# One attention chain across the token groups, with values and scores taking turns on TensorE

## The chip, the cores and the metric

The kernel runs on one core of one Trainium2 chip. The metric is the device time of one execution in microseconds (us); what is compared is the median over several executions.

## What is computed

Three layers follow one another, all in float32. The attention is cut into chunks of 64 tokens, so each chunk of each head sees only itself; its output feeds a dense mixture of 4 experts, and that feeds a mixture of 8 experts in which each token takes one expert.

```python
# q, k, v: (4, 8, 576, 64), cut along the sequence into chunks of 64
scores = scale * np.matmul(q_c, k_c.transpose(0, 1, 2, 4, 3))
scores = scores - np.max(scores, axis=-1, keepdims=True)
attn = np.exp(scores)
attn = attn / (np.sum(attn, axis=-1, keepdims=True) + 1e-09)
out = np.matmul(attn, v_c)
...
x = attn_out.transpose(0, 2, 1, 3).reshape(B * S, H * D)      # 2304 tokens x 512
x = _moe_ref(x=x, **moe_kwargs)        # 4 experts, all tokens through each, weighted
return _moe2_ref(x=x, **moe2_kwargs)   # 8 experts, each token through the one it scores highest
```

## The kernel before

The 2304 tokens are 18 tiles of 128 tokens, and a tile holds two chunks of 64. The tiles form seven groups of 2, 3, 3, 3, 3, 2 and 2 (`GROUPS`). The first mixture works group by group: for each expert it takes eight steps (`chunk`), each of which multiplies the group's tokens with one 128-wide slice of the hidden layer (`ffn1`, L358 to L360) and then, for the step before, with the second weight matrix (`ffn2`, L418). Every float32 operand there is split into a high and a low part, which is why each product appears three times. Two groups share one pass over the weights (`SUPER`), so the steps run in the order group 0, then 1 and 2, then 3, then 4 and 5, then 6.

The attention of a group is done in pieces that are put between these steps. For one tile the pieces are:

- scores (`att_scores`, L186): 8 heads times 2 chunks, 16 matmuls of 64x64x64. The two chunks lie on the two halves of the partitions, so their operands and results use either partitions 0 to 63 or 64 to 127. All results go to one PSUM bank. VectorE then takes the maximum (L192) and subtracts it (L193), and ScalarE exponentiates (L197).
- normalisation (`att_norm`, L202 to L206): VectorE alone.
- transposes (`att_transpose`, L214): four 128x128 transposes into one PSUM bank, copied out by ScalarE (L216, `aT`).
- values (`att_values`, L237): again 16 matmuls of 64x64x64 into one PSUM bank; ScalarE copies the result out as `xh` (L244), VectorE makes the rest `xl` (L245). When a tile's values are done its input buffer is free, and the load of the tile four further on is queued for two steps later.

Scores, transposes and values all take their bank from one ring of two PSUM banks (`ps("m")`), in the order of the program. `att_pieces(g)` lists the pieces of group g. For all groups but the first, a piece can hold the values of tile i-2 (all 16 matmuls) followed by the scores of tile i (all 16), then come the transposes of tile i-1, then the normalisation of tile i. At the start of a group there are no values to go with the scores of its first two tiles, and at its end no scores to go with the values of its last two: a group of n tiles has n+2 such pieces. `plan` spreads the pieces of a group evenly over at most 24 steps that end just before the group is first needed. Group 0 has a list of its own, done before the first step. A piece that is the first of its step stands on TensorE between that step's `ffn1` and the `ffn2` of the step before; a further piece of the same step comes after that `ffn2`.

Of the kernel before, what the change touches and what calls it, by code (L numbers as in the profile page):

```python
# [1 line left out]

# [15 lines left out]
P = 128  # L18
NT = 2304
NTILE = NT // P  # L20
# [7 lines left out]
CH = 64  # L28
# [28 lines left out]
def attn_moe_moe2(ctx, tc, att, probs, wg, wgt, w12, m2w, out):  # L57
# [17 lines left out]
    def ps(tag):  # L75
        return ring(psum, "ps_" + tag, {"h": 2, "o": 4, "m": 2}[tag], [P, 512], F32)
# [89 lines left out]
    def heads(t, half):  # L166

        if t < GROUPS[0]:
            return slice(4 * half, 4 * half + 4), 4
        return (slice(0, H), H) if half else None  # L170

    def att_scores(t, half):

        a = atin[t]
        if half == 0:
            live[t] = [
                sds[t % 2],
                apool.tile([P, 2, H], F32, tag="mx", name=f"mx{t}"),
                None,
            ]  # L180
        if half == 0 or t < GROUPS[0]:
            live[t][2] = ps("m").rearrange("p (h x) -> p h x", x=CH)
        sd, mx, sc = live[t]
        for g in range(4 * half, 4 * half + 4):
            for c in (slice(0, CH), slice(CH, P)):
                nc.tensor.matmul(  # L186
                    sc[c, g, :], lhsT=a[c, 512 + g * CH:512 + (g + 1) * CH], rhs=a[c, g * CH:(g + 1) * CH],
                    start=True, stop=True,
                )
        if heads(t, half):  # L190
            hs, n = heads(t, half)
            nc.vector.tensor_reduce(out=mx[:, 0, hs].unsqueeze(2), in_=sc[:, hs, :], axis=AX.X, op=ALU.max)  # L192
            nc.vector.tensor_tensor(  # L193
                out=sd[:, hs, 0:CH], in0=sc[:, hs, :], in1=mx[:, 0, hs].unsqueeze(2).to_broadcast([P, n, CH]),
                op=ALU.subtract,
            )
            nc.scalar.activation(sd[:, hs, 0:CH], sd[:, hs, 0:CH], AF.Exp, scale=0.125)  # L197

    def att_norm(t, half):
        sd, mx, _ = live[t]  # L200
        hs, n = heads(t, half)
        nc.vector.tensor_reduce(out=mx[:, 1, hs].unsqueeze(2), in_=sd[:, hs, :], axis=AX.X, op=ALU.add)  # L202
        nc.vector.reciprocal(mx[:, 1, hs], mx[:, 1, hs])
        if hs.start == 0:
            live[t][2] = apool.tile([P, H, CH], F32, tag="pn", name=f"pn{t}")
        nc.vector.tensor_tensor(  # L206
            out=live[t][2][:, hs, :], in0=sd[:, hs, 0:CH], in1=mx[:, 1, hs].unsqueeze(2).to_broadcast([P, n, CH]), op=ALU.mult
        )

    def att_transpose(t):  # L210
        sdf = live[t][2].rearrange("p h k -> p (h k)")
        pt = ps("o" if t < GROUPS[0] else "m")
        for i in range(4):
            nc.tensor.transpose(pt[:, i * P:(i + 1) * P], sdf[:, i * P:(i + 1) * P], ident)  # L214
        aT = apool.tile([P, 512], F32, tag="aT", name=f"aT{t}")
        nc.scalar.copy(aT, pt)  # L216
        live[t] = aT

    def att_values(t, half, g):
        a = atin[t]  # L220
        if g not in xs:
            n = GROUPS[g] * P
            xs[g] = (
                xpool.tile([P, KD, n], F32R, tag="xh", name=f"xh{g}"),
                xpool.tile([P, KD, n], F32R, tag="xl", name=f"xl{g}"),
            )
        xh, xl = xs[g]
        off = (t - starts[g]) * P
        if half == 0:
            live[t] = [live[t], None]  # L230
        if half == 0 or t < GROUPS[0]:
            live[t][1] = ps("o" if t < GROUPS[0] else "m")
        aT, pv = live[t]
        for q in range(4 * half, 4 * half + 4):
            w = slice(q * CH, (q + 1) * CH)
            for c in (slice(0, CH), slice(CH, P)):
                nc.tensor.matmul(  # L237
                    pv[c, w], lhsT=a[c, 1024 + q * CH:1024 + (q + 1) * CH], rhs=aT[c, w], start=True, stop=True,
                )
        if heads(t, half):  # L240
            hs, n = heads(t, half)
            ks = slice(hs.start // 2, hs.stop // 2)
            pvv = pv.rearrange("p (k x) -> p k x", x=P)[:, ks, :]
            nc.scalar.copy(xh[:, ks, off:off + P], pvv)  # L244
            nc.vector.tensor_tensor(out=xl[:, ks, off:off + P], in0=pvv, in1=xh[:, ks, off:off + P].bitcast(F32),  # L245
                                    op=ALU.subtract)
        if half == 1:
            live.pop(t)
            atin.pop(t)
            if t + NATT < NTILE:  # L250
                attq.append((t + NATT, stream["call"] + 2 if stream["call"] else 0))

    def att_pieces(g):

        a = starts[g]
        n = GROUPS[g]
        S = lambda i, h: (lambda: att_scores(a + i, h))
        N = lambda i, h: (lambda: att_norm(a + i, h))
        T = lambda i: (lambda: att_transpose(a + i))
        V = lambda i, h: (lambda: att_values(a + i, h, g))  # L260
        if g == 0:
            return [S(0, 0), S(0, 1), N(0, 0), S(1, 0), N(0, 1), S(1, 1), T(0), N(1, 0), N(1, 1), V(0, 0), V(0, 1),
                    T(1), V(1, 0), V(1, 1)]


        pcs = []
        for i in range(n + 2):
            both = []
            if i >= 2:
                both += [V(i - 2, 0), V(i - 2, 1)]  # L270
            if i < n:
                both += [S(i, 0), S(i, 1)]
            pcs.append(lambda both=both: [p() for p in both])
            if 1 <= i <= n:
                pcs.append(T(i - 1))
            if i < n:
                pcs.append(N(i, 1))
        return pcs


# [592 lines left out]
    for g in range(1, len(GROUPS)):  # L873
        free = lastuse[g - NX] + 2 if g >= NX else 0
        end = first[g] - (1 if g < len(GROUPS) - 1 else KF + 1)
        begin = max(at, free, end - 24)
        pcs = att_pieces(g)
        for i, p in enumerate(pcs):
            plan.setdefault(begin + i * (end - begin) // len(pcs), []).append(p)
        at = end  # L880
# [40 lines left out]
    for t in range(3, NATT):  # L921
        att_load(t)
    pieces = att_pieces(0)

    warm = zero.bitcast(BF16)[:, 0:512]
# [117 lines left out]
def _layouts(q, k, v, moe_domain_probs, moe_w1, moe_w2, moe2_w_gate, moe2_w1, moe2_w2):  # L1043
# [16 lines left out]
    def chunks(w1, w2):  # L1060
        n = w1.shape[0]
        a = w1.reshape(n, KD, P, KF, P).transpose(0, 3, 2, 1, 4).reshape(n, KF, P, KD * P)
        return np.concatenate([a, w2.reshape(n, KF, P, D)], axis=-1)

    return [att, probs, wg, moe2_w_gate.T, chunks(moe_w1, moe_w2), chunks(moe2_w1, moe2_w2)]

# [17 lines left out]
```

## Time and profile before

| | |
|---|---|
| median of 3 executions | 1174.14 us (1174.12 to 1174.23) |
| the profiled execution, its own time | 1172.4 us |
| its span, first to last instruction | 1170.3 us |
| mean granted TensorE clock | 0.998 |
| TensorE (PE) busy | 1146.9 us, 98% of the span |
| VectorE (DVE) busy | 694.1 us, 59% |
| ScalarE (ACT) busy | 480.6 us, 41% |

The profile is one execution, seen by the hardware profiler. PE is TensorE's matmul row and PEld its weight loads, which run beside matmuls. An instruction is named by its line in the kernel, its engine, its operation and `out<-in`; `64*64 64x64` for a matmul means 64 rows and 64 columns of the array in use and 64 columns streamed. A float32 matmul shows as two records, each a weight load and a matmul, so the 16 matmuls of one tile's scores are 32 records. Matmul records overlap, since their ends are modelled; the distance from one start to the next is what TensorE takes for one.

### The profile page before, as it was taken

To read this page: it belongs to the slowest core of one execution; us is meant where nothing else is said; L and a number is where in the kernel's file an instruction comes from. 1 tells how busy PE (TensorE), PEld (TensorE's weight loads), DVE (VectorE), ACT (ScalarE), POOL (GpSimd) and SP (SyncE) were. 2 spreads that over 40 slices of the span, in tenths; PEclk is the share of its full clock that TensorE was granted. 3 is DMA by queue.
4 is the path that set the end of the run, shared out by engine and by line. 5 is a ranking of instruction groups with operands and counts; after the bars stand their busy time and mean duration, and the time that the engine had idled before them with its cause. 6 is when DMAs were issued, how large, how long until landed. Compare 5 with 4: busy or idle time off the path is not lost. (4 is left out here: it accounts for less than half of the span.)

```text
span 1170.3 us, 19108 instructions
## 1 busy us (share of the span) xinstructions
PE 1146.9 (98%) x7447; PEld 1027.7 (88%) x7447; DVE 694.1 (59%) x1370; ACT 480.6 (41%) x801; POOL 97.6 (8%) x125
## 2 busy tenths in 40 slices
PE   6999999999999999999999999999999999999996
PEld 5998899999999999988899999988898899888885
DVE  6766735233443666667363746266866765788872
ACT  5544323131221334333141414145445555677771
POOL 0000000000000000100010001001102211222220
PEclk9999999999999999999999999999999999999999
DMA  8657513031131443444031304046763586686850
GB/s 321 202 204 289 190 44 127 2 108 37 54 117 55 156 139 120 137 152 159 22 110 36 126 19 127 21 159 178 200 245 126 202 319 214 203 279 241 288 205 18
DMA packets 52293, 174.14 MB, mean 149 GB/s; under 512 B 10718, under 2 KB 11358, under 8 KB 52064
## 3 DMA queue, kind: packets, MB, share of 16 engines
q1 hardware_dynamic: 46240, 156.54, 39.8%
q0 software_dynamic: 5952, 16.28, 4.1%
q8 instruction: 61, 1.00, 0.4%
q14 instruction: 40, 0.33, 0.1%
HBM read 162.61 MB, written 11.36 MB: 149 GB/s over the span
## 5 line engine op out<-in xcount | busy, mean ns | idle before, releaser
L364 DVE SCALAR_TENSOR_TENSOR hl<-ps_h,hh 128x256 fp32r<-128x256 f32 (+1 forms) x272 | 132.3, 486 | 360.4 <-ACT hh L363 355.6
L363 ACT ACTIVATE hh<-ps_h 128x256 fp32r<-128x256 f32 (+1 forms) x272 | 118.2, 434 | 544.7 <-PE ps_h L360 537.2
L418 PE MATMUL ps_o<-wh,hh 128*128 128x512 f32 x840 | 325.5, 398 | 0.0
L418 PE MATMUL ps_o<-wl,hh 128*128 128x512 f32 (+1 forms) x784 | 305.8, 391 | 0.0
L317 DVE TENSOR_TENSOR wl<-raw,wh 128x1024 fp32r<-128x1024 f32 x212 | 259.3, 1223 | 57.8 <-ACT wh L316 56.8
L358 PE MATMUL ps_h<-xh,wh 128*128 128x384 f32 (+1 forms) x896 | 282.8, 316 | 0.0
L360 PE MATMUL ps_h<-xh,wl 128*128 128x384 f32 (+1 forms) x896 | 280.7, 313 | 0.8 <-DVE wl L317 0.8
L359 PE MATMUL ps_h<-xl,wh 128*128 128x384 f32 (+1 forms) x896 | 280.7, 313 | 0.6 <-DVE xl L245 0.5
L418 PE MATMUL ps_o<-wh,hl 128*128 128x512 f32 x672 | 262.2, 390 | 0.0
L316 ACT CAST wh<-raw 128x1024 fp32r<-128x1024 f32 x212 | 220.7, 1042 | 4.0 <-DMA raw<-in_w 4.0
L418 PEld LDWEIGHTS ps_o<-wh,hh 128*128 128x128 f32 x840 | 157.7, 188 | 25.9 <-ACT x L783 0.5
L358 PEld LDWEIGHTS ps_h<-xh,wh 128*128 128x128 f32 x896 | 168.3, 188 | 9.7 <-DVE wl L317 0.4
L359 PEld LDWEIGHTS ps_h<-xl,wh 128*128 128x128 f32 x896 | 168.3, 188 | 9.0 <-DVE xl L245 1.0
L360 PEld LDWEIGHTS ps_h<-xh,wl 128*128 128x128 f32 x896 | 168.3, 188 | 1.0 <-DVE wl L317 1.0
L418 PEld LDWEIGHTS ps_o<-wl,hh 128*128 128x128 f32 (+1 forms) x784 | 144.5, 184 | 20.1
L418 PEld LDWEIGHTS ps_o<-wh,hl 128*128 128x128 f32 x672 | 126.1, 188 | 27.5
L375 PE MATMUL ps_h<-x,wh 128*128 128x384 f32 x224 | 66.6, 357 | 0.8 <-ACTq L1031 0.8
L471 DVE CUSTOM_DVE_ANT_0 junk<-y,wgb 128x512 bf16<-128x512 f32 x96 | 65.7, 684 | 0.1
L358 PE MATMUL ps_h<-x,wh 128*128 128x256 f32 x192 | 54.6, 284 | 1.8 <-DVEq L1031 1.6
L376 PE MATMUL ps_h<-x,wl 128*128 128x192 f32 x224 | 56.1, 250 | 0.0
L360 PE MATMUL ps_h<-x,wl 128*128 128x256 f32 x192 | 53.9, 281 | 0.0
L359 PE MATMUL ps_h<-x,wh 128*128 128x256 f32 x192 | 53.9, 281 | 0.0
(187 smaller groups left out, 916.2 us busy)
## 6 DMA issues: line engine op xcount, KB each, us to landing
raw<-in_w SPq DMA_DIRECT2D x160, 512.0 KB
raw<-in_m2w SPq DMA_DIRECT2D x52, 512.0 KB
raw_xh<-in_m2w SPq DMA_DIRECT2D x27, 512.0 KB
raw_xl<-in_m2w SPq DMA_DIRECT2D x27, 512.0 KB
atin<-in_att SPq DMA_DIRECT2D x16, 768.0 KB
ytok<-y POOLq DMA_DIRECT2D x18, 256.0 KB, 3.4
wgb<-in_wgt SPq DMA_DIRECT2D x1, 2048.0 KB
atin<-in_att SPq DMA_DIRECT2D x4, 256.0 KB
```

The source lines that it names most:

```text
L316: nc.scalar.copy(wh, raw)
L317: lows.append(lambda: nc.vector.tensor_tensor(out=wl, in0=raw, in1=wh.bitcast(F32), op=ALU.subtract))
L358: nc.tensor.matmul(hp[:, :n], lhsT=w_h, rhs=xh(k), start=(k == 0), stop=False)
L359: nc.tensor.matmul(hp[:, :n], lhsT=w_h, rhs=xl(k), start=False, stop=False)
L360: nc.tensor.matmul(hp[:, :n], lhsT=w_l, rhs=xh(k), start=False, stop=(k == KD - 1))
L363: nc.scalar.activation(hh, hp[:, :n], AF.Relu)
L364: nc.vector.scalar_tensor_tensor(out=hl, in0=hp[:, :n], scalar=0.0, in1=hh.bitcast(F32), op0=ALU.max, op1=ALU.subtract)
L375: nc.tensor.matmul(hp[:, :2 * n], lhsT=wh[:, c], rhs=x[:, k, :, :n], start=(k == 0), stop=False)
L376: nc.tensor.matmul(hp[:, :n], lhsT=wl[:, c], rhs=x[:, k, 0, :n], start=False, stop=(k == KD - 1))
L418: nc.tensor.matmul(y, lhsT=l, rhs=r, start=(fc == 0 and q == 0), stop=(fc == KF - 1 and q == len(parts) - 1))
L471: nc.vector.tensor_tensor_reduce(out=junk, in0=tiles[i], in1=wgb[:, e, :], scale=1.0, scalar=0.0, op0=ALU.mult, op1=ALU.add, accum_out=lg[ ...
```

## The change

Three things change. The group boundary goes: `att_pieces` now lists, for tile i of a group, its transposes, the normalisation of tile i+1, and one piece with the values of tile i and the scores of tile i+2, whether or not tile i+2 belongs to the next group. Group 1 starts the chain with the scores of its first two tiles alone; the last two tiles of all have values alone. Inside such a piece, values and scores are generators that take turns: two matmuls of values (one on each half of the partitions), then two of scores, eight times, and only then the instructions on the other engines, those of the values first. And the scores of a chunk that sits on partitions 0 to 63 are written to partitions 64 to 127 of their bank, and the other way round; the values undo this by reading the other one of each pair of 64-wide columns of `aT` (`q ^ 1`).

```diff
+    def other(c):
+        return slice(P - c.stop, P - c.start)
+
+    def run(*parts):
+        parts = list(parts)
+        while parts:
+            for p in list(parts):
+                try:
+                    next(p)
+                except StopIteration:
+                    parts.remove(p)
...
                 nc.tensor.matmul(
-                    sc[c, g, :], lhsT=a[c, 512 + g * CH:512 + (g + 1) * CH], rhs=a[c, g * CH:(g + 1) * CH],
+                    sc[other(c), g, :], lhsT=a[c, 512 + g * CH:512 + (g + 1) * CH], rhs=a[c, g * CH:(g + 1) * CH],
                     start=True, stop=True,
                 )
+            yield
...
         for q in range(4 * half, 4 * half + 4):
-            w = slice(q * CH, (q + 1) * CH)
+            w, r = [slice(i * CH, (i + 1) * CH) for i in (q, q ^ 1)]
             for c in (slice(0, CH), slice(CH, P)):
                 nc.tensor.matmul(
-                    pv[c, w], lhsT=a[c, 1024 + q * CH:1024 + (q + 1) * CH], rhs=aT[c, w], start=True, stop=True,
+                    pv[c, w], lhsT=a[c, 1024 + q * CH:1024 + (q + 1) * CH], rhs=aT[c, r], start=True, stop=True,
                 )
+            yield
...
-        S = lambda i, h: (lambda: att_scores(a + i, h))
+        S = lambda i, h: (lambda: run(att_scores(a + i, h)))
+        S8 = lambda i: joined(att_scores(a + i, 0), att_scores(a + i, 1))
+        V8 = lambda i: joined(att_values(a + i, 0, g), att_values(a + i, 1, g))
-        V = lambda i, h: (lambda: att_values(a + i, h, g))
+        V = lambda i, h: (lambda: run(att_values(a + i, h, g)))
...
-        pcs = []
-        for i in range(n + 2):
-            both = []
-            if i >= 2:
-                both += [V(i - 2, 0), V(i - 2, 1)]
-            if i < n:
-                both += [S(i, 0), S(i, 1)]
-            pcs.append(lambda both=both: [p() for p in both])
-            if 1 <= i <= n:
-                pcs.append(T(i - 1))
-            if i < n:
-                pcs.append(N(i, 1))
+        pcs = [lambda: run(S8(0)), N(0, 1), lambda: run(S8(1))] if g == 1 else []
+        for i in range(n):
+            pcs.append(T(i))
+            if a + i + 1 < NTILE:
+                pcs.append(N(i + 1, 1))
+            pcs.append(lambda i=i: run(V8(i), *([S8(i + 2)] if a + i + 2 < NTILE else [])))
         return pcs
```

(`joined` is `itertools.chain`.)

## Rows read from the trace of the kernel before

**Rows 1.** The page, busy time by engine: us, share of the span, instructions.
```profile
PE 1146.9 (98%) x7447; PEld 1027.7 (88%) x7447; DVE 694.1 (59%) x1370; ACT 480.6 (41%) x801; POOL 97.6 (8%) x125
```
**Rows 2.** Waits of TensorE from 20 to 760 us: total, times, longest.
```profile
PE ps_h L360 <- DVE wl L317: 0.8, 1, 0.8
```
**Rows 3.** The ps_m tile's instructions, 20 to 760 us: scores and values.
```profile
L186 PE MATMUL ps_m<-atin x512: 218/218/267, 38.0 to 682.6; 64*64 64x64 f32 x171
L237 PE MATMUL ps_m<-aT,atin x512: 218/218/267, 68.9 to 737.7; 64*64 64x64 f32 x171
```
**Rows 4.** Timeline of TensorE around scores alone: start us, us, instruction.
```profile
37.34 0.28 PE L359 MATMUL ps_h<-xl,wh 128*128 128x256 f32 x1
...
37.80 0.28 PE L360 MATMUL ps_h<-xh,wl 128*128 128x256 f32 x1
38.01 1.15 PE L186 MATMUL ps_m<-atin 64*64 64x64 f32 x32
...
39.42 0.40 PE L418 MATMUL ps_o<-wl,hh 128*128 128x512 f32 x1
```
**Rows 5.** Timeline of TensorE around values alone.
```profile
90.87 0.28 PE L360 MATMUL ps_h<-xh,wl 128*128 128x256 f32 x1
91.08 1.15 PE L237 MATMUL ps_m<-aT,atin 64*64 64x64 f32 x32
...
92.49 0.40 PE L418 MATMUL ps_o<-wl,hh 128*128 128x512 f32 x1
```
**Rows 6.** Timeline of TensorE around values followed by scores.
```profile
68.69 0.28 PE L360 MATMUL ps_h<-xh,wl 128*128 128x256 f32 x1
68.90 1.15 PE L237 MATMUL ps_m<-aT,atin 64*64 64x64 f32 x32
69.88 1.10 PE L186 MATMUL ps_m<-atin 64*64 64x64 f32 x32
70.91 0.50 PE L418 MATMUL ps_o<-wh,hh 128*128 128x512 f32 x1
71.24 0.40 PE L418 MATMUL ps_o<-wl,hh 128*128 128x512 f32 x1
...
72.17 0.39 PE L418 MATMUL ps_o<-wh,hl 128*128 128x512 f32 x1
```
**Rows 7.** Windows, scores (L186) alone, group 3: window, length, busy and records, clock.
```profile
286.50:288.50 2.00, 1.15 (x32) 1.01 (x32) 1.00 0.00 0
...
331.00:334.00 3.00, 1.10 (x32) 1.02 (x32) 1.00 0.54 180
```
**Rows 8.** Windows, values (L237) alone, group 3.
```profile
331.00:334.00 3.00, 1.15 (x32) 1.01 (x32) 1.00 0.54 180
...
381.00:384.00 3.00, 1.15 (x32) 1.01 (x32) 1.00 0.49 175
```
**Rows 9.** Weight loads begun by 38.06, by 38.11, by 38.13 us (three timelines).
```profile
38.01 0.14 PEld L186 LDWEIGHTS ps_m<-atin 64*64 64x64 f32 x2
...
38.01 0.19 PEld L186 LDWEIGHTS ps_m<-atin 64*64 64x64 f32 x4
...
38.01 0.25 PEld L186 LDWEIGHTS ps_m<-atin 64*64 64x64 f32 x6
```
**Rows 10.** Timeline, float32 matmuls of the logits: one place in the array.
```profile
768.80 1.89 PE L457 MATMUL ps_m<-yT,wg_sb 128*8 128x256 f32 x8
```
**Rows 11.** Timeline of group 2: values, their copies, and the next transposes.
```profile
127.12 1.15 PE L237 MATMUL ps_m<-aT,atin 64*64 64x64 f32 x32
...
128.61 0.59 ACT L244 CAST xh<-ps_m 128x512 fp32r<-128x512 f32 x1
...
130.10 1.22 DVE L317 TENSOR_TENSOR wl<-raw,wh 128x1024 fp32r<-128x1024 f32 x1
...
131.23 0.69 DVE L245 TENSOR_TENSOR xl<-ps_m,xh 128x512 fp32r<-128x512 f32 x1
...
133.43 0.60 PE L214 MATMUL ps_m<-ident,pn 128*128 128x128 f32 x4
```

More of the change, by code (lines that the diff above doesn't have):

```diff
@@ L1 @@
 from contextlib import ExitStack
+from itertools import chain as joined
 import concourse.bass as bass
```

## The prediction

> **What bounds the kernel now.** I read the busy times first: TensorE is busy for 98% of the span, the next engine for 59% [rows 1]. Then the waits of TensorE over the stretch that holds all attention pieces between the steps, 20 to 760 us: one wait, 0.8 us, for a weight [rows 2]. So there TensorE goes from one instruction to the next without waiting for any engine or transfer, and the time moves only by what its own instructions take. Shorter work on VectorE, ScalarE or the queues gives nothing.
>
> Then I counted the attention's matmuls in that stretch. Scores and values have 512 records each [rows 3], 32 for a tile, so 16 tiles of each (group 0's two come earlier). The question is how they are bundled. I call an unbroken stretch of 64x64 matmuls a run. By the code a group of n tiles has n+2 runs; in group 3 the windows show it: scores alone first, scores and values together once in the middle, values alone at the end [rows 7, 8]. Over groups 1 to 6 that is 16 + 6 x 2 = 28 runs: 12 with scores alone, 12 with values alone, 4 with both.
>
> **What a run costs.** From the start of the last `ffn1` matmul before a run to the start of the second `ffn2` matmul after it (the first is drawn out, 0.50 against 0.40), scores alone take 39.42 - 37.80 = 1.62 us [rows 4], values alone 92.49 - 90.87 = 1.62 us [rows 5], both 71.24 - 68.69 = 2.55 us [rows 6]. In each stand two neighbours that run anyway: one `ffn1` matmul, (37.80 - 37.34) / 4 = 0.115 us [rows 4], and one `ffn2` matmul, (72.17 - 71.24) / 4 = 0.233 us [rows 6], together 0.35. So a run costs 1.27 us with one kind and 2.20 us with both. The second kind adds 0.93 us for 16 matmuls, 0.058 us each; what is left of a lone run, 1.27 - 0.93 = 0.34 us, is the price of going from 128x128 to 64x64 matmuls and back: the gap before the first, the longer tail of the last, the drawn-out `ffn2` matmul. It is paid once per run, whatever the run holds.
>
> The Trainium skill, TensorEngine Tiling (Array Packing), Key Properties, says that a change of tiling mode drains TensorE while a change of tile doesn't; by that rule the price per run stays a price per run when more tiles are used in it, and the trace agrees, since values followed by scores pay 0.34 us once [rows 6].
>
> **The change part by part.**
>
> *One chain.* The new list has 3 + 3n pieces for group 1 and 3n for the others, less what the last two tiles lack. Scores alone remain for the first two tiles of group 1, values alone for the last two tiles of group 6, and 14 runs hold both: 18 runs for 28. In `plan` no two of them fall into one step, and none stands next to another. The instructions stay the same in number: 512 score records, 512 value records, 64 transposes. Ten runs fewer at 0.34 us is 3.4 us. As a check: before 24 x 1.27 + 4 x 2.20 = 39.3 us, after 4 x 1.27 + 14 x 2.20 = 35.9 us.
>
> *Turns and the other half.* Before, consecutive matmuls alternate between two quarters of the array: rows and columns 0 to 63, rows and columns 64 to 127. After, the scores use the two other quarters, so the order is V0, V1, S0, S1 over four quarters. Could they overlap more than now? A matmul is two records on one quarter. Two float32 records after each other on one place of the array can't overlap: eight records of 256 columns take 1.89 us [rows 10], at most 0.236 each, so 0.059 for 64 columns. The pace now, 0.058 per matmul of two records, is about one such record: the second record of one matmul already overlaps the first of the next, on the other quarter. What holds the third record back? Two weight loads start at 38.01, the third and fourth not before 38.06 [rows 9], though the third goes to a half of the array in which nothing of this run is loaded or running. It waits behind the second, which waits for the first on its own quarter. So records are taken in order, and each matmul costs one record's time because of its own two records, however many quarters are free. With four quarters nothing of that changes. I take 0.058 us as before, so 0.
>
> The bounds: if matmuls of four quarters did overlap fully, 32 matmuls would take the 0.93 us of 16; if only the part above one record's stream went (0.058 to about 0.053), 14 x 32 x 0.005 = 2.2 us would. On the other side stands the second rival below.
>
> *Instructions moved.* The copies of the values (`xh`, `xl`) now follow the scores' matmuls too, so they can start up to 0.93 us later. In group 2, where pieces are densest, the values' matmuls begin at 127.12 and end some 1 us later; ScalarE takes `xh` at 128.61 only, since it is busy with a weight, and VectorE takes `xl` at 131.23, behind a weight's rest of 1.22 us begun at 130.10 [rows 11]. With both kinds done at about 129.0, `xh` moves by some 0.4 us to about 129.6 and `xl` stays where it is. What needs that bank next is the transposes' matmul at 133.43, 1.5 us after `xl` ends at 131.92. Cost 0; without that cover (one more weight's rest in front, 1.22 us, on top of 0.93) it would be about 0.65 us, at the two or three places of group 2 where the transposes come one step after values.
>
> *Loads and the earlier scores.* The scores of a group's first two tiles move into the group before. They need input that was loaded after the values four tiles earlier; in the densest stretch, group 2, the pieces of a tile are three steps apart, a load has at least three steps of some 4 us each, and no wait of TensorE for such a load stands in the stretch now [rows 2]. Group 1's stretch gets two more tiles of scores and group 6's two fewer; other engines have the room (VectorE 59%, ScalarE 41% [rows 1]). Cost 0, at the worst a microsecond at one place. Group 0 keeps its order; its scores change the quarter alone: 0.
>
> Sum: -3.4 us.
>
> **The rivals.**
>
> 1. *Four quarters at once.* If the order on TensorE isn't what holds the pace, the 14 mixed runs go from 2.20 towards 1.27 us: 14 x 0.93 = 13.0 us more, 16.4 in all, 1157.7 us; half of it 1164.2 us. For it: the change puts four matmuls on four different quarters, each with a bank that no matmul of the same columns writes. Against it: the order of the loads [rows 9] and the fit of 0.058 to one record. The skill's page named above says under Key Properties that tiles work independently, loads and matmuls in parallel, which would give this time; TensorE: Matmul & The Clock Gate, Part 3, says that matmuls start and end strictly in order, and by that the pace stays. The order of the loads [rows 9] sides with the latter. Chance 0.15.
>
> 2. *Quarters that share columns don't overlap.* Now the overlapping pair, V0 and V1, shares neither rows nor columns. After the change V1 and S0 share columns 64 to 127, S1 and the next V0 columns 0 to 63. The trace has no such pair. If they had to follow one another, each of the 15 changes of kind in a mixed run would lose the overlap of a record, 0.05 us: 14 x 15 x 0.05 = 10.5 us, less 3.4 gained: 1181.2 us. It decides from 3.4 / 210 = 0.016 us for a change of kind on; below that the kernel is still faster. Against it: they write different banks, since values and scores take the two banks of the ring in turn. Chance 0.10 for enough to be slower than before or even with it. Were every change of quarter a change of shape at 0.34 us, it would be 210 x 0.34 = 71 us; values and scores show no gap between them now [rows 6], but they sit on the same quarters. I give that 0.01 within the 0.10.
>
> 3. *The gain is eaten by waits.* The late copies or an input that isn't there stop TensorE: two or three places at 0.65 us and one load at 1 us, together 1 to 3 us, so 1171.7 to 1173.7 us. Against it: the slack of 1.5 us above. Chance 0.08.
>
> The rest, 0.67, is my forecast. That fewer runs result is certain by the list; only their price could differ, and it is the same in the three places shown.
>
> **How the numbers follow.** The profiled execution took 1172.4 us with a span of 1170.3; the sum makes that 1169.0 and 1166.9. The median of the runs shown is 1174.14, 1.7 us above the profiled execution, and the same 3.4 us bring it to 1170.7. The range: below, the forecast with the 0.005 us per matmul gone, 1168.3; above, most of the third rival, 1173.5. Outside it lie most of the first rival (0.12) and of the second (0.08), so it holds 0.80. No change that could be told from the measurement is 0.2%, 2.3 us: 1171.8 to 1176.5. Faster than that are the forecast but for a sliver and the first rival, 0.79; the same are most of the third and the mild part of the second, 0.12; slower is the rest of the second, 0.09.
>
> **What the profile after would show.** Right: 18 runs between the steps; a lone run still 1.62 us by the measure above; a mixed run, from the last `ffn1` to the second `ffn2` matmul, 2.55 us; weight loads in twos some 0.058 us apart; no new wait of TensorE; a span near 1167. Wrong: a mixed run near 1.62 us (first rival) or over 3 us (second); a wait of the transposes for `xl`, or of scores for their input (third); off the attention, any stage that has moved.

## The result and the profile after

The changed kernel takes 1158.29 us (median of 4 executions, 1157.21 to 1160.22) against 1174.13 us before: a ratio of 0.9875, 95% interval 0.9863 to 0.9887. That is 15.8 us less where 3.4 were forecast, below the range; the first rival, four quarters at once, had been given 1157.7 us. The profiled execution took 1160.22 us, its span is 1158.5 us.

TensorE is still the bound, with as many instructions, and less busy by the difference (page, busy time by engine, against [rows 1]):

```profile
PE 1134.3 (98%) x7447; PEld 1016.8 (88%) x7447; DVE 693.1 (60%) x1370; ACT 479.6 (41%) x801; POOL 98.1 (8%) x125
```

A run of one kind is what it was. This is the timeline of TensorE around scores alone, against [rows 4]: 42.17 - 40.55 = 1.62 us.

```profile
40.55 0.28 PE L374 MATMUL ps_h<-xh,wl 128*128 128x256 f32 x1
40.75 1.15 PE L202 MATMUL ps_m<-atin 64*64 64x64 f32 x32
...
42.17 0.40 PE L432 MATMUL ps_o<-wl,hh 128*128 128x512 f32 x1
```

A mixed run is not. The same view, against [rows 6] (values are now L254, scores L202):

```profile
71.43 0.28 PE L374 MATMUL ps_h<-xh,wl 128*128 128x256 f32 x1
71.64 0.28 PE L254 MATMUL ps_m<-aT,atin 64*64 64x64 f32 x2
71.65 0.27 PE L202 MATMUL ps_m<-atin 64*64 64x64 f32 x2
71.75 0.22 PE L254 MATMUL ps_m<-aT,atin 64*64 64x64 f32 x2
71.76 0.23 PE L202 MATMUL ps_m<-atin 64*64 64x64 f32 x2
...
72.56 0.23 PE L254 MATMUL ps_m<-aT,atin 64*64 64x64 f32 x2
72.58 0.22 PE L202 MATMUL ps_m<-atin 64*64 64x64 f32 x2
72.73 0.50 PE L432 MATMUL ps_o<-wh,hh 128*128 128x512 f32 x1
73.07 0.40 PE L432 MATMUL ps_o<-wl,hh 128*128 128x512 f32 x1
```

From the last `ffn1` to the second `ffn2` matmul it is 73.07 - 71.43 = 1.64 us, 1.29 us without the two neighbours' 0.35, where two kinds took 2.20. 32 matmuls now take what 16 took. The rows show how: two records of values and two of scores start within 0.02 us, the next four 0.11 us later, and from then on four more every 0.06 us. A turn of values is two matmuls and so four records in the program, yet only two start before the scores do: the first records of four matmuls on four quarters go together, and then the four second ones.

Over all, 4 x 1.27 + 14 x 1.29 = 23.1 us stand in the place of 39.3: 16.2 us less. Not all of it arrives. These are all waits of TensorE from 20 to 760 us, against [rows 2]. The second is new; the third is group 0's, at 21.90 us, which fell ahead of 20 us in the kernel before:

```profile
PE ps_h L374 <- DVE wl L331: 0.8, 1, 0.8
PE ps_o L432 <- DVE y L445: 0.5, 3, 0.2
PE ps_h L373 <- DVE xl L263: 0.2, 1, 0.2
```

By the starts of the matmuls (below, with e13) each of the three waits for `y` costs 0.42 us, 1.3 us in all: at the first, two steps from one matmul of L432 to the next take 334.62 - 333.73 = 0.89 us where 0.47 is usual. The matmul that waits is late by 0.32, and the one behind it by 0.10 more.

The spans of the two profiled executions differ by less than that, 1170.3 - 1158.5 = 11.8 us. Most of what is missing there, 3.2 us, is the start, whose order the change leaves as it was. In the profiled execution of the changed kernel the first expert step began at 20.29 us:

```profile
12.90 1.97 PE L254 MATMUL ps_o<-aT,atin 64*64 64x64 f32 x32 [1.02 <-ACT aT L233]
...
20.29 0.58 PE L372 MATMUL ps_h<-xh,wh 128*128 128x256 f32 x1
```

In another profile of the same kernel (run e9 below) it began at 17.08, as in the kernel before:

```profile
12.56 1.15 PE L254 MATMUL ps_o<-aT,atin 64*64 64x64 f32 x32 [1.02 <-ACT aT L233]
...
17.08 0.38 PE L372 MATMUL ps_h<-xh,wh 128*128 128x256 f32 x1
```

The same 32 records took 1.97 us in the one and 1.15 in the other. This goes with TensorE's clock. In the profile that starts late, the trace's first record of the granted clock, at its higher level (2.4 GHz), is at 21.1 us, and the first matmuls of `ffn1` stand 0.21 us apart up to there (20.67, 20.88, 21.10) and 0.115 us behind it; in e9 that record is at 11.7 us. In the profiles of this study the first step starts between 16.3 and 20.3 us. To compare kernels without that I use the stretch from the first matmul of the expert steps to the first matmul of the logits on TensorE (768.80 us before): 751.72 us before, 736.38 after. That is 15.3 us less; 16.2 less 1.3 for the new waits is 14.9. Of the 0.4 us between, 0.3 is group 0's wait for `xl`, which is shorter after a late start: from the first matmul of the steps to the one that waits it is 21.90 - 20.29 = 1.61 us, against 1.93 before.

### The profile page after: what moved, and what is told of

Same layout as the page of the kernel before. It is cut to its first block, busy times and chain, and to the rows that moved or that the text cites. A ratio compares the mean times of both kernels' runs of the same rounds, so it can differ in the third digit from the quotient of the medians.

```text
span 1158.5 us, 19097 instructions
## 1 busy us (share of the span) xinstructions
PE 1134.3 (98%) x7447; PEld 1016.8 (88%) x7447; DVE 693.1 (60%) x1370; ACT 479.6 (41%) x801; POOL 98.1 (8%) x125
## 5 line engine op out<-in xcount | busy, mean ns | idle before, releaser
L432 PE MATMUL ps_o<-wh,hh 128*128 128x512 f32 x840 | 325.1, 398 | 0.5 <-DVE y L445 0.5
L432 PE MATMUL ps_o<-wl,hh 128*128 128x512 f32 (+1 forms) x784 | 305.9, 392 | 0.0
L432 PE MATMUL ps_o<-wh,hl 128*128 128x512 f32 x672 | 262.4, 391 | 0.0
L432 PEld LDWEIGHTS ps_o<-wh,hh 128*128 128x128 f32 x840 | 157.8, 188 | 27.1 <-DVE y L445 1.8
L432 PEld LDWEIGHTS ps_o<-wl,hh 128*128 128x128 f32 (+1 forms) x784 | 144.6, 184 | 19.7
L432 PEld LDWEIGHTS ps_o<-wh,hl 128*128 128x128 f32 x672 | 126.2, 188 | 27.4
```

The source lines that it names most:

```text
L432: nc.tensor.matmul(y, lhsT=l, rhs=r, start=(fc == 0 and q == 0), stop=(fc == KF - 1 and q == len(parts) - 1))
```

## The experiments

I compare two theories. By the first, each quarter of the array takes its own records at 0.058 us each and doesn't wait for the others, as long as the matmuls stand near each other in the program. By its rival, the one of the prediction, records are taken in order, and the gain has another source: the longer chain, the turns on whatever quarters, or the other half as such. In the table the mixed run is the first one of a profile, without the neighbours' 0.35 us; the stretch is the one just defined, from one profile; medians are beside the kernel before on the same chip. e5 to e8 were timed once each, so what is read from them is their profiles, in which the 14 mixed runs agree (beside groups of three tiles they measure 0.06 us more, since an `ffn1` matmul is longer there).

| run | mixed run, us | stretch, us | median, us (executions) | before, us | ratio, 95% interval |
|---|---|---|---|---|---|
| before | 2.20 | 751.72 | | 1174.13 | |
| after | 1.29 | 736.38 | 1158.29 (4) | 1174.13 | 0.9875, 0.9863 to 0.9887 |
| e1 chain only | 2.20 | 749.07 | 1170.11 (10) | 1172.96 | 0.9973, 0.9958 to 0.9987 |
| e2 turns and other half only | 1.28 | 747.95 | 1169.58 (8) | 1172.96 | 0.9972, 0.9959 to 0.9984 |
| e3 own half | 2.21 | 749.19 | 1171.19 (10) | 1172.96 | 0.9982, 0.9971 to 0.9993 |
| e4 no turns | 2.03 | 747.07 | 1168.28 (5) | 1172.96 | 0.9959, 0.9945 to 0.9973 |
| e5 turns of 4 | 1.33 | 737.41 | 1157.05 (1) | 1172.76 | |
| e6 turns of 8 | 1.69 | 742.10 | 1164.40 (1) | 1172.76 | |
| e7 shared rows | 2.12 | 751.04 | 1174.53 (1) | 1172.76 | |
| e8 shared columns | 2.13 | 751.29 | 1172.72 (1) | 1172.76 | |
| e9 changed again | 1.28 | 736.69 | 1157.45 (4) | 1172.33 | 0.9870, 0.9856 to 0.9885 |
| e10 paired ends | 1.28 | 734.11 | 1155.78 (5) | 1172.33 | 0.9853, 0.9839 to 0.9866 |
| e11 warm start | 1.29 | 737.88 | 1158.66 (4) | 1172.33 | 0.9872, 0.9855 to 0.9889 |
| e12 both | 1.28 | 734.14 | 1154.48 (5) | 1172.33 | 0.9853, 0.9836 to 0.9870 |
| e13 late norm | 1.29 | 735.32 | 1155.61 (5) | 1174.24 | 0.9848, 0.9828 to 0.9868 |
| e14 paired, late norm | 1.29 | 732.55 | 1154.97 (5) | 1174.24 | 0.9834, 0.9817 to 0.9852 |

### One part at a time

**e1**, the chain alone:

```diff
-                    sc[other(c), g, :], lhsT=...
+                    sc[c, g, :], lhsT=...
...
-            w, r = [slice(i * CH, (i + 1) * CH) for i in (q, q ^ 1)]
+            w, r = [slice(i * CH, (i + 1) * CH) for i in (q, q)]
...
-            pcs.append(lambda i=i: run(V8(i), *([S8(i + 2)] if a + i + 2 < NTILE else [])))
+            pcs.append(lambda i=i: [run(p) for p in [V8(i)] + ([S8(i + 2)] if a + i + 2 < NTILE else [])])
```

> The one chain alone: 18 runs for 28, values and then scores in a mixed run, scores on their own half. Quarters theory (each quarter of the array takes its own records at 0.058 us each and doesn't wait for the others; only matmuls that stand near each other on different quarters overlap): a mixed run stays at 2.20 us, 3.4 us less than before in all, about 1170.7 us. Rival (the longer chain itself brings the gain, by later loads or fewer changes of shape than counted): about 1158 us, with mixed runs of 2.20 us.

The runs number 18, and a mixed run is what it was in the kernel before:

```profile
70.76 0.28 PE L374 MATMUL ps_h<-xh,wl 128*128 128x256 f32 x1
70.97 1.15 PE L254 MATMUL ps_m<-aT,atin 64*64 64x64 f32 x32
71.95 1.10 PE L202 MATMUL ps_m<-atin 64*64 64x64 f32 x32
...
73.31 0.40 PE L432 MATMUL ps_o<-wl,hh 128*128 128x512 f32 x1
```

The stretch is 2.65 us shorter. 3.4 less the same three waits for y, which this kernel has too, is 2.1; this profile starts late (19.67 us), which gives 0.3 as above, and some 0.2 us are not accounted for. So the chain brings both the 3.4 us that the prediction gave it and the waits.

**e2**, the old list by groups with turns and the other half:

```diff
...
+        pcs = []
+        for i in range(n + 2):
+            pcs.append(lambda i=i: run(*([V8(i - 2)] if i >= 2 else []), *([S8(i)] if i < n else [])))
+            if 1 <= i <= n:
+                pcs.append(T(i - 1))
+            if i < n:
+                pcs.append(N(i, 1))
```

> Turns and the other half in the old list by groups: 28 runs, 4 of them mixed. Quarters theory: the 4 mixed runs go from 2.20 to 1.28 us, 3.7 us less than before, about 1170.4 us. Rival (the chain brings the gain): within 1 us of the kernel before.

Four mixed runs of 1.28 us; the stretch is 3.77 us shorter, 4 x 0.92 = 3.7. The waits for y are not there.

**e3**, the changed kernel with the first two edits of e1 (scores on their own half), turns kept:

> Chain and turns, but the scores on their own half, so that values and scores use the same two quarters. Quarters theory: a mixed run is 2.20 us, the whole about 1170.7 us. Rival (turns between two banks or two kinds of operands are what matters, on whatever quarters): a mixed run of 1.28 us, the whole about 1158 us.

```profile
70.89 0.28 PE L374 MATMUL ps_h<-xh,wl 128*128 128x256 f32 x1
71.10 0.33 PE L254 MATMUL ps_m<-aT,atin 64*64 64x64 f32 x4
71.27 0.28 PE L202 MATMUL ps_m<-atin 64*64 64x64 f32 x4
71.38 0.28 PE L254 MATMUL ps_m<-aT,atin 64*64 64x64 f32 x4
...
73.45 0.40 PE L432 MATMUL ps_o<-wl,hh 128*128 128x512 f32 x1
```

Turns on the same two quarters give nothing: 2.56 us by the measure from `ffn1` to `ffn2`. Here the records do come in fours of one kind, as the program has them. What matters is that the scores sit on other quarters.

**e4**, the changed kernel with the third edit of e1 (other half, all values before all scores):

> Chain and the other half, but all 16 matmuls of values before all 16 of scores. Quarters theory with a short reach: 2.20 us for a mixed run, about 1170.7 us in all; with a reach over 16 matmuls (TensorE's queue lets the scores start while values wait): down to 1.28 us and 1158 us. In between: as far as the reach goes, each pair of matmuls that overlap at the seam saves 0.058 us.

```profile
69.14 0.28 PE L374 MATMUL ps_h<-xh,wl 128*128 128x256 f32 x1
69.34 0.97 PE L254 MATMUL ps_m<-aT,atin 64*64 64x64 f32 x26
70.11 0.27 PE L202 MATMUL ps_m<-atin 64*64 64x64 f32 x2
70.15 0.28 PE L254 MATMUL ps_m<-aT,atin 64*64 64x64 f32 x3
...
70.28 0.98 PE L202 MATMUL ps_m<-atin 64*64 64x64 f32 x27
...
71.52 0.40 PE L432 MATMUL ps_o<-wl,hh 128*128 128x512 f32 x1
```

This is the row that settles it. 26 records of values have started when the first two of scores start at 70.11; the other six values, which the program has ahead of all scores, start after them. So records on free quarters go ahead of records that wait for theirs, but only over a short reach: 0.17 us are saved, three places of 0.058, at the one change of kind.

### How far ahead, and which quarters

**e5** and **e6** lengthen the turns of the changed kernel from two matmuls to four and eight:

```diff
                 try:
-                    next(p)
+                    for _ in range(2):        # e6: 4
+                        next(p)
```

> As the changed kernel, but in turns of four matmuls instead of two. Without turns the scores began while 6 records (3 matmuls) of values were still to start, and a mixed run was 2.04 us, 0.17 shorter than on two quarters. Reach theory (at each change of kind three places of 0.058 us are saved, as far as there is something to overlap with): with 7 changes of kind nearly all is overlapped, 1.28 to 1.40 us. Rival (the seam is a matter of the end of a run alone, and turns must be no longer than one pair): near 2.0 us.

> The same in turns of eight: 3 changes of kind, 3 x 0.17 = 0.5 us saved by the reach theory, a mixed run of about 1.70 us. Rival: near 2.0 us.

```profile
68.38 0.28 PE L375 MATMUL ps_h<-xh,wl 128*128 128x256 f32 x1
68.58 0.27 PE L255 MATMUL ps_m<-aT,atin 64*64 64x64 f32 x2
68.61 0.27 PE L203 MATMUL ps_m<-atin 64*64 64x64 f32 x2
...
70.06 0.40 PE L433 MATMUL ps_o<-wl,hh 128*128 128x512 f32 x1
```

A mixed run is 1.33 (e5, above) and 1.69 us (e6). Three changes of kind at 0.17 us make 2.20 - 0.51 = 1.69, so e4's reach holds at every change; with turns of four it covers nearly all. The first scores show the same reach directly: they start when six records of the first turn of values are still to start, behind 2 of its 8 in e5, behind 10 of its 16 in e6, and behind 26 of 32 in e4.

**e7** and **e8** take all heads of one chunk and then all of the other, so that only two quarters are in use at a time:

```diff
-        for g in range(4 * half, 4 * half + 4):
-            for c in (slice(0, CH), slice(CH, P)):
...
+        both = (slice(0, CH), slice(CH, P))
...
+            todo = [(g, both[half]) for g in range(H)]  # e8, scores: both[1 - half]
+        for k, (g, c) in enumerate(todo):               # values the same with q; yield after every second
...
```

> Turns and the other half as in the changed kernel, but each tile takes all 8 heads of the first chunk and then all 8 of the second, so that in a mixed run the two quarters in use at a time share their rows (operands on partitions 0 to 63, later 64 to 127) and differ in columns. Quarters theory (each quarter for itself): 16 records on each of two quarters, then again, 2 x 0.93 + 0.34 = 2.20 us for a mixed run, or some 0.17 less where the halves meet; a lone run is the same 2.0 to 2.2 us, against 1.27. Rival (quarters that share rows wait for one another): 4 x 0.93 + 0.34 = 4.1 us for a mixed run.

> The same, but the scores begin with the second chunk, so that the two quarters in use at a time share their columns (results on partitions 0 to 63, later 64 to 127, in two banks) and differ in rows. Quarters theory: 2.0 to 2.2 us for a mixed run. Rival (quarters that share columns wait for one another, the second rival of the prediction): 4.1 us.

Mixed runs of e7 and of e8:

```profile
72.47 0.28 PE L382 MATMUL ps_h<-xh,wl 128*128 128x256 f32 x1
...
74.94 0.39 PE L440 MATMUL ps_o<-wl,hh 128*128 128x512 f32 x1
```

```profile
71.24 0.28 PE L382 MATMUL ps_h<-xh,wl 128*128 128x256 f32 x1
...
73.72 0.39 PE L440 MATMUL ps_o<-wl,hh 128*128 128x512 f32 x1
```

Two quarters with the same rows, or with the same columns (and results in two banks), overlap as well as two that share nothing: 2.12 and 2.13 us, where 2.20 is the run on two quarters before. And a lone run, now on one quarter at a time, shows what a quarter alone does: 32 records in 1.90 us where two quarters took 1.15 (e7, scores alone; 2.02 against 1.27 us without the neighbours).

```profile
40.25 1.90 PE L204 MATMUL ps_m<-atin 64*64 64x64 f32 x32
```

Its weight loads begin one at a time, some 0.06 us apart, where on two quarters they begin two at a time [rows 9]. These are the loads begun by 40.30 and by 40.33 us (two timelines):

```profile
40.25 0.13 PEld L204 LDWEIGHTS ps_m<-atin 64*64 64x64 f32 x1
...
40.25 0.19 PEld L204 LDWEIGHTS ps_m<-atin 64*64 64x64 f32 x2
```

So the limit is each quarter's own stream of records, and nothing that quarters share is seen to cost anything here.

### The size, the start and what is left

**e9** is the changed kernel once more.

> The changed kernel itself once more, for its size beside the kernel before on the same chip. By the runs of 64x64 matmuls (14 x 0.92 us from the four quarters, 3.4 us from the chain) 16.3 us less than before, ratio 0.986. What differs from that is the start: in the profiles so far the full clock was granted between 8 and 21 us after the first instruction, and the first expert step began between 16.9 and 20.3 us; times should spread by about these 3 us, for either kernel.

14.9 us less than before on that chip, where 16.3 were expected: that sum left out the three waits for y. The executions ran from 1156.38 to 1158.33, those of the kernel before from 1171.12 to 1174.60, so they spread by 2.0 and 3.5 us. The stretch is 736.69 us, 15.0 less than before, close to the 14.9 of the sum with the waits.

**e10** pairs the four lone runs:

```diff
-        pcs = [lambda: run(S8(0)), N(0, 1), lambda: run(S8(1))] if g == 1 else []
+        pcs = [lambda: run(S8(0), S8(1)), N(0, 1)] if g == 1 else []
...
+            if a + i == NTILE - 1:
+                pcs.append(lambda i=i: run(V8(i - 1), V8(i)))
+                continue
```

The scores of tile 3 go to their own half, and the results of the last tile's values to the other half, from which ScalarE copies them back.

> The changed kernel with its four lone runs made into two: the scores of the first two tiles of group 1 take turns (the second tile's on its own half, so that all four quarters are used), and so do the values of the last two tiles (the last one's results go to the other half and are copied back through an extra buffer). Quarters theory: each pair goes from 2 x 1.27 to 1.28 us, 2.5 us less than the changed kernel, 16 runs in all, about 1155.5 us. Rival (scores with scores, or values with values, overlap less, or the later copies stop TensorE): 1157 to 1158 us.

Scores with scores (below) take 1.64 us by the measure from `ffn1` to `ffn2`, 1.29 without the neighbours, and values with values 1.28 us: what one kind took before. Sixteen runs are left; the stretch is 2.3 to 2.6 us shorter than in the two profiles of the changed kernel, as expected; the median is 1.7 us lower than that of e9, with intervals that overlap.

```profile
38.34 0.28 PE L384 MATMUL ps_h<-xh,wl 128*128 128x256 f32 x1
38.55 1.16 PE L202 MATMUL ps_m<-atin 64*64 64x64 f32 x64
...
39.98 0.40 PE L442 MATMUL ps_o<-wl,hh 128*128 128x512 f32 x1
```

**e11** and **e12** put more matmuls on zeros into the gaps of the start, alone and together with e10:

```diff
-WARM = (0, 0, 0, 0, 0, 0, 2, 0, 0, 0, 0, 0, 4, 0, 0)
+WARM = (6, 0, 3, 0, 0, 0, 2, 2, 0, 0, 0, 0, 4, 0, 0)
```

> The changed kernel with 11 more matmuls on zeros in TensorE's gaps before the first expert step (6 before the first scores, 3 after the first half of them, 2 after the first transposes). If the spread of the times is the time at which the full clock is granted, it comes earlier and at about the same place in each execution: the first expert step starts near 17 us, the median falls by 1 to 2 us and the spread shrinks below 1.5 us. If the spread comes from elsewhere (loads at the start), no change, or slower by the added matmuls where they delay real work, up to 1 us.

> The two edits together: the sum of what each gives, about 1154 us if both do what their theories say, 1155.5 us if the added matmuls do nothing.

In these two profiles the trace's first record of the full clock is at 6.4 and 5.0 us, and the first expert step did start at 16.3 and 16.4 us, but the executions spread no less (1155.94 to 1159.94, and 1153.23 to 1158.63), and the medians are not told apart from e9 and e10. So the start is not the whole of the spread. The profiles show two more parts. One is TensorE's wait for gathered token rows (`yb`) near 1000 us, which is 0.6 us long in e10's profile and 2.3 in e1's. The other is seen in e11's profile alone, in the windows (length, busy and records of each engine, then the granted clock, the share of the DMA engines and GB/s): the clock falls to 0.51, the lower of its two levels (1.2 GHz), for 3.4 us near 1003 us, after a stretch in which TensorE was busy for 6.0 of 8 us and stood still for 2.0 us for `yb`. In e1 the wait of 2.3 us was not followed by such a fall. e11 also has a wait of 0.9 us for `hl` at 28.27 us that no other profile has, most of the 1.2 us by which its stretch is longer than e9's. What else the spread is made of, and what brings these on, stays open.

```profile
995.00:1003.00 8.00, 5.98 (x38) 5.20 (x37) 6.48 (x16) 5.41 (x11) 1.41 (x1) 1.00 0.98 312
1003.00:1006.40 3.40, 3.40 (x12) 2.40 (x11) 1.36 (x3) 0.58 (x1) 0.00 (x0) 0.51 0.29 117
```

**e13** and **e14** go after the three waits, in the changed kernel and in e10. In the changed kernel the sum of an expert's results (L445) stands on VectorE behind a normalisation (L219 to L223) that is the first piece of its step:

```profile
331.91 0.69 DVE L219 TENSOR_REDUCE mx<-sd 128x8 f32<-128x520 f32 x1
...
332.88 0.69 DVE L223 TENSOR_TENSOR pn<-sd,mx 128x512 f32<-128x512 f32 x1
...
333.48 2.06 DVE L445 SCALAR_TENSOR_TENSOR y<-ps_o,pr,y 128x512 f32<-128x512 f32 x3
...
333.73 0.39 PE L432 MATMUL ps_o<-wh,hl 128*128 128x512 f32 x1
...
334.28 0.50 PE L432 MATMUL ps_o<-wh,hh 128*128 128x512 f32 x1 [0.17 <-DVE y L445]
...
334.62 0.40 PE L432 MATMUL ps_o<-wl,hh 128*128 128x512 f32 x1
```

The edit puts each such normalisation at the later place of its step (but for the first of the chain, which is listed apart):

```diff
-                pcs.append(N(i + 1, 1))
+                pcs.append([N(i + 1, 1)])
...
-            plan.setdefault(begin + i * (end - begin) // len(pcs), []).append(p)
+            at_step = plan.setdefault(begin + i * (end - begin) // len(pcs), [])
+            if isinstance(p, list):
+                if not at_step:
+                    at_step.append(lambda: None)
+                p = p[0]
+            at_step.append(p)
```

> The changed kernel, with each normalisation that is first in its step put behind the second matmuls of the step before and what hangs on them. In the profile of the changed kernel TensorE has three waits that the kernel before has not (near 334, 473 and 509 us, 0.32 us each by the distance of the matmuls), each for the sum of an expert's results (y), which stands on VectorE behind a normalisation. If that order is the cause, the three waits go and 1.0 us with them, about 1156.5 us. Rival (VectorE is late there for its other work): the waits stay, no change.

> The same edit in the kernel with its lone runs paired: 2.5 us by the pairs and 1.0 us by the waits less than the changed kernel, about 1154 us; by the rival 1155 us.

In e13 the sum now goes first on VectorE:

```profile
328.52 2.06 DVE L445 SCALAR_TENSOR_TENSOR y<-ps_o,pr,y 128x512 f32<-128x512 f32 x3
330.50 0.69 DVE L219 TENSOR_REDUCE mx<-sd 128x8 f32<-128x520 f32 x1
```

and from 20 to 740 us TensorE has one wait left, the one of the kernel before:

```profile
PE ps_h L374 <- DVE wl L331: 0.8, 1, 0.8
```

The stretch is 735.32 us, 16.4 less than before, where the runs alone make 16.2: with the waits gone the count of runs is whole. It is 1.4 us shorter than e9's, so the waits cost nearer to 1.3 than to the 1.0 us of the expectation, which counted only the matmul that waits and not the late one behind it. e14, with 732.55 us of stretch and a ratio of 0.9834, has the shortest of both and is faster than the kernel before and than the changed one (0.9875); its interval, 0.9817 to 0.9852, lies below that of the changed kernel.

## Why the prediction was wrong

**One chain.** Right: 18 runs, a lone run still 1.62 us by the measure, and e1 with 3.4 us less from the runs. What the step missed is the wait for y, 1.3 us, which every kernel with the chain has until the normalisations are moved (e13, e14), and which e2 has not.

**Turns and the other half.** This is the step that failed: "records are taken in order, and each matmul costs one record's time because of its own two records, however many quarters are free". The price taken was 0, the measured one 14 x 0.92 = 12.8 us. It came from a misreading of [rows 9]. The two weight loads that start together at 38.01 were taken for the two records of one matmul, and so the third load, 0.05 us later, for one that goes to an idle half and waits in order. They are the first records of two matmuls on two quarters, which had both been idle, and the next two are their second records, each waiting for its own quarter: on one quarter alone (e7) no two loads begin together. Read so, the rows say that a quarter with nothing to do is served at once, ahead of records that wait. Rows with a line number could not tell the two readings apart, since both chunks' matmuls stand on one line; with values and scores on two lines the profile after shows it, and e4 shows it across 16 matmuls. The fit of 0.058 us to one record's stream was right, and it holds for either reading: a matmul costs two records on its quarter, and two quarters make that one record each. What shows it is e7, with one record every 0.058 us on one quarter; [rows 10] give only an upper bound. The lower end of the range counted on 0.053 us for a record, which no row shows, and by its own sum it is 1168.5 us and not 1168.3.

The Trainium skill, TensorE: Matmul & The Clock Gate, Part 3, says that matmuls start and end strictly in program order; the rows of e4 show matmuls of scores that start ahead of six records of values issued before them, so here the measurement decides against it as far as starts go (ends are modelled). The Trainium skill, TensorEngine Tiling (Array Packing), Key Properties, has different tiles load weights and multiply in parallel, and the trace agrees: 32 matmuls on four quarters take 1.29 us, 16 on two 1.27.

**Instructions moved, loads.** The copies of the values cost nothing, and no load was late: no wait for either is new. The normalisations were not looked at as moved instructions, though the new list puts them into other steps.

**The rivals.** The first was right in mechanism and size, 16.4 us less against 16.2 by the runs; its chance of 0.15 was too low, since what spoke against it was one view of six loads. The second fell: V1 with S0 and S1 with V0 share columns and overlap, and e8 shows it for a whole run. The third was right in kind, 1.3 us of waits, at another place and for another reason than named.

## What to carry to other kernels

Small float32 matmuls whose rows and columns fit a quarter of the array (64x64x64 here) are worth putting on all four quarters, and near each other in the program: turns of two to four matmuls, so that a matmul on a free quarter is never far behind one that waits. Where a view shows two instructions of one line starting together, ask which two they are before an order is inferred from them, and look for a second reading that fits as well. And when pieces are spread over steps by a count, changing the count moves every piece: look at each in-order engine for what it now stands in front of.

## What the runs showed of the hardware

- Float32 matmuls of 64x64x64 take 0.058 us per record on each quarter of the array, and quarters don't slow each other: 32 matmuls on four took 1.29 us, 16 on two 1.27 us, the changes of shape included.
- Records on a free quarter start ahead of earlier ones that wait for theirs, about three matmuls (six records) ahead: 0.17 us saved at each change of kind where the turns are longer than that (e4, e6).
- Quarters that share rows, or columns (with results in different banks), overlap as well as those that share neither: 2.12, 2.13 and 2.20 us (e7, e8, e1).
